# Two packed attentions and a gated convolution: transposes of batches 0 and 1 on TensorE, low words on VectorE, one more column for the 1e-9

## The chip, the cores and the metric

The kernel runs on one core of a Trainium2 chip. The metric is the device time of the program in microseconds, the median of the timed runs. Five engines work beside each other, each through its own queue in order: TensorE (PE in the profile, its weight loads PEld), VectorE (DVE), ScalarE (ACT), GpSimd (POOL) and SyncE (SP), which issues all transfers here. Work waits for other engines through semaphores.

## The reference

```python
def _attn_ref(q, k, v, p):
    scale = 1.0 / np.sqrt(q.shape[-1])
    def sm_attn(qq, kk, vv):
        s = scale * np.matmul(qq, kk.transpose(0, 1, 3, 2))
        s = s - np.max(s, axis=-1, keepdims=True)
        a = np.exp(s)
        a = a / (np.sum(a, axis=-1, keepdims=True) + 1e-09)
        return np.matmul(a, vv)
    p_packed = sm_attn(p, k, v)
    return sm_attn(q, p_packed, p_packed)

def _moe_ref(x, w_val, conv_w, w_out):       # x: (batch, seq, heads * head_dim)
    ...
    for k in range(K):                       # K = 5 taps, causal
        gate_pre += conv_w[k][None, None, :] * xp[:, k:k + S, :]
    gate = 1.0 / (1.0 + np.exp(-gate_pre))
    return (gate * (x @ w_val) @ w_out)
```

q, k, v are (8 batches, 8 heads, 576 rows, 64), p is (8, 8, 32, 64), all float32. In the first attention the 32 rows of p ask k and v; in the second the 576 rows of q ask the 32 packed rows. The result, 576 by 512 for each batch, goes through a convolution of 5 taps and a sigmoid as the gate, times the product with `w_val`, and then through `w_out`. The three weights come as float64.

## The kernel before

Each batch goes through the same stages, each written as a generator that issues a few instructions and yields: `k` (`keys`: p and k turned so that head_dim lies on partitions), `a` (`attn_pack`: scores `s`, maximum `nb`, exponentials `a`, their transposes `at`, the product `pv` with v, and the packed rows `ppd`), `q` (`queries`), `p` (`packed_turned`: `ppT`), `s` (`attn_out`: scores, turned on VectorE to `t`, maximum `mx` over 32 packed rows, subtracted on GpSimd, exponential on ScalarE), `t` (`weighted`: sums, reciprocals `rs`, scaling on GpSimd, turned back to `a` of the second attention, split into a high part `a2h` and a low part `a2l`), `w` (`packed_values`: packed rows times `w_val`, split into `wph` and `wpl`), `x` (`mixed`: for batches 0 to 2 the whole convolution on TensorE with the tap products `kx`, for the others the attention's output `xp`), `g` (`gate`: for batches 3 to 7 four taps on VectorE, then tanh on ScalarE, into `sig`), `v` (`value`: `val` on TensorE, times the gate on VectorE, split into `gvh` on ScalarE and `gvl` on GpSimd) and `o` (`project`: the output `o` of 128 rows in 12 matmuls, evicted to `osb` and stored).

Capital letters are loads (`K`, `Q`, `V`, `P`, and `L` for the weights) and the weights' preparation: `from_double` takes the words of a float64 apart on ScalarE, VectorE and GpSimd; `W` makes `wv`, `O` makes `woh` and `wol`, `C` the taps `cw` and their spread form `cwb`.

What is issued in which order is a table of tokens, `ORDER` (lines 48 to 71): `a2.2` takes two steps of batch 2's `attn_pack`. The class `InOrder` (lines 74 to 95) keeps each engine's instructions in that order. So an engine stands still when the first instruction of its queue waits, whatever is behind it. The `|` in the table marks where the buffers for the weights' words are given up and `gvh` and `gvl` take their place; 3 PSUM tiles (`big`) of two banks serve scores, transposes and values, and one bank each `mid` and `out`.

k and q are turned by VectorE in blocks of 32 by 32, two instructions of 1152 columns for each; so head_dim is split in two halves of 32, and a score is two matmuls of 32 rows that accumulate:

```python
                            of(rows, j, h),
                            xT[j // 2][rows, j % 2, :, h, :],
                            start=(h == 0),
                            stop=(h == 1),
```

The 1e-9 is added to each sum by VectorE (line 468), from a constant tile `eps`.

## Time and profile before

| | us |
|---|---|
| timed runs | 299.49, 299.0, 297.74; median 299.0 |
| the profiled execution | 301.0 |
| its span, first to last instruction | 299.2 |
| busy: PE, PEld, DVE, ACT, POOL | 259.6, 192.0, 245.2, 164.4, 124.6 |
| mean granted clock of TensorE | 0.945 |
| read from HBM, written | 33.57 MB, 9.44 MB |

In the rows of the profile, `L82` is the line of the helper that issues all instructions, so the tiles' names tell the groups apart. A row of a group has the engine, the operation, output<-inputs, the shapes, the count, the busy time with the mean of one in ns, and the engine's idle time before them with what ended it. A row in order of time has the start and the duration in us; `x12` is 12 instructions in one row. An instruction's duration can contain the time in which it was held up.

### The profile page before, as it was taken

What the parts mean: (1) busy time and instruction counts of PE and PEld (TensorE: products, weight loads), DVE (VectorE), ACT (ScalarE), POOL (GpSimd) and SP (SyncE); (2) the same over time, 40 slices, a digit from 0 to 9 for tenths busy, and PEclk for the clock granted to TensorE, in tenths of its full rate; (3) what the DMA queues carried; (4) which work ended last, traced back from release to release, by engine and by line L of the source; (5) the groups of instructions that cost most, each with busy time, mean ns of one, the idle gap of its engine ahead of it and who ended that gap; (6) DMA issues with size and microseconds to landing.
All of it is one profiled execution on the core that took longest, in us unless ns stands there. A gap on an engine that the chain in (4) does not pass through costs nothing.

```text
span 299.2 us, 8542 instructions
## 1 busy us (share of the span) xinstructions
PE 259.6 (87%) x3676; PEld 192.0 (64%) x3676; DVE 245.2 (82%) x349; ACT 164.4 (55%) x306; POOL 124.6 (42%) x107
## 2 busy tenths in 40 slices
PE   0465555989999998999999999999999979999984
PEld 0143343457677874768776768867876758778852
DVE  1499569799977898687999999999999989847841
ACT  4155345576753564477573766657764637546412
POOL 1334358659916474314424741541522803511230
PEclk9998555899999999999999999999999979999998
DMA  7999996534952498355467511565010101111004
GB/s 219 303 334 265 271 278 200 149 84 157 290 160 70 142 298 226 95 144 156 139 169 196 184 37 46 184 163 183 37 71 37 38 35 70 62 45 70 35 2 175
DMA packets 25839, 43.56 MB, mean 146 GB/s; under 512 B 5829, under 2 KB 11973, under 8 KB 25802
## 3 DMA queue, kind: packets, MB, share of 16 engines
q1 hardware_dynamic: 25802, 43.02, 48.6%
q8 instruction: 29, 0.48, 0.7%
q14 instruction: 8, 0.07, 0.1%
HBM read 33.57 MB, written 9.44 MB: 144 GB/s over the span
## 4 chain that ended last, share of the span: by engine, by line
PE 56%; DVE 23%; DMA 9%; ACT 5%; issue 3%; SPq 2%; POOL 1%; POOLq 1%; ACTq 0%; DVEq 0%
PE o L82 23%; DVE sig L82 13%; PE val L82 11%; PE x L82 8%; PE s L82 5%; DMA vm<-in_v_dram 3%; PE pv L82 3%; DMA wo_words<-in_moe_w_out_dram 3%; PE at L82 3%; DMA km<-in_k_dram 2%; DVE sm L82 2%; DVE kT L82 2%; SPq L82 2%; PE wp L82 1%; ACT sig L82 1%
## 5 line engine op out<-in xcount | busy, mean ns | idle before, releaser
L82 DVE SCALAR_TENSOR_TENSOR sig<-xp,cw,sig 128x576 f32<-128x576 f32 x80 | 76.5, 957 | 8.7 <-ACT sig L82 7.2
L82 POOL TENSOR_TENSOR gvl<-sig,gvh 128x576 fp32r<-128x576 f32 x32 | 48.4, 1514 | 79.7 <-ACT gvh L82 79.7
L82 PE MATMUL o<-woh,gvh 128*128 128x512 f32 x144 | 59.0, 410 | 2.8 <-ACT osb L82 2.7
L82 PE MATMUL o<-woh,gvl 128*128 128x512 f32 x144 | 57.3, 398 | 1.0 <-POOL gvl L82 1.0
L82 PE MATMUL o<-wol,gvh 128*128 128x512 f32 x144 | 56.9, 395 | 0.0
L82 PE MATMUL val<-a2h,wph 128*128 128x288 f32 x128 | 39.6, 310 | 0.0
L82 PE MATMUL val<-a2h,wpl 128*128 128x288 f32 x128 | 37.8, 295 | 0.0
L82 PE MATMUL val<-a2l,wph 128*128 128x288 f32 x128 | 37.7, 294 | 0.0
L82 ACT COPY osb<-o 128x512 f32<-128x512 f32 x34 | 19.9, 587 | 31.4 <-PE o L82 25.2
L82 PEld LDWEIGHTS o<-woh,gvh 128*128 128x128 f32 x144 | 27.4, 190 | 15.0 <-ACT osb L82 6.3
L82 PEld LDWEIGHTS o<-woh,gvl 128*128 128x128 f32 x144 | 27.3, 190 | 8.3 <-POOL gvl L82 2.1
L82 DVE SCALAR_TENSOR_TENSOR sig<-sig,val 128x576 f32<-128x576 f32 x32 | 23.7, 740 | 9.9 <-PE val L82 5.6
L82 PEld LDWEIGHTS o<-wol,gvh 128*128 128x128 f32 x144 | 27.5, 191 | 4.8
L82 POOL TENSOR_TENSOR t<-t,mx 128x576 f32<-128x576 f32 x16 | 20.8, 1299 | 19.5 <-DVE mx L82 19.4
L82 PE MATMUL pv<-vm,a1t 96*32 96x64 f32 x768 | 16.7, 239 | 13.9 <-ACT a1t L82 8.0
L82 POOL TENSOR_TENSOR t<-t,rs 128x576 f32<-128x576 f32 x16 | 20.6, 1288 | 17.7 <-DVE rs L82 15.0
L82 PEld LDWEIGHTS pv<-vm,a1t 96*32 96x32 f32 x768 | 13.4, 121 | 22.5 <-ACT a1t L82 14.4
L82 PE MATMUL s<-kT,pT 32*32 32x288 f32 x512 | 17.2, 479 | 12.1 <-DVE kT L82 11.7
L82 ACT CAST gvh<-sig 128x576 fp32r<-128x576 f32 x32 | 21.5, 673 | 10.5 <-DVE sig L82 9.4
L82 PEld LDWEIGHTS val<-a2h,wph 128*128 128x128 f32 x128 | 24.1, 188 | 5.0 <-DVE sig L82 1.4
L82 PEld LDWEIGHTS val<-a2h,wpl 128*128 128x128 f32 x128 | 24.1, 188 | 0.4
L82 PEld LDWEIGHTS val<-a2l,wph 128*128 128x128 f32 x128 | 24.1, 188 | 0.0
(81 smaller groups left out, 457.7 us busy)
## 6 DMA issues: line engine op xcount, KB each, us to landing
km<-in_k_dram SPq DMA_DIRECT2D x16, 576.0 KB, 6.1
vm<-in_v_dram SPq DMA_DIRECT2D x16, 576.0 KB, 7.1
qm<-in_q_dram SPq DMA_DIRECT2D x16, 576.0 KB, 5.3
out_dram<-osb SPq DMA_DIRECT2D x36, 256.0 KB, 2.1
wv_words<-in_moe_w_val_dram SPq DMA_DIRECT2D x4, 512.0 KB, 5.9
wo_words<-in_moe_w_out_dram SPq DMA_DIRECT2D x4, 512.0 KB, 10.2
p<-in_p_dram SPq DMA_DIRECT2D x16, 64.0 KB, 3.5
cw_words<-in_moe_conv_w_dram SPq DMA_DIRECT2D x1, 20.0 KB
```

What stands on the lines that cost most here:

```text
L82: made = getattr(self.engine, op)(*args, **kw)
```

## The change

It has six parts.

1. k, q and p of batches 0 and 1 (`BY_PE`) are loaded over all 128 partitions, 16 partitions for each head and one packet of 4608 B for each partition, and turned by TensorE: 3 groups of 12 transposes for each tensor into a `big` PSUM tile, each group copied to the two tiles `kT` or `qT` by two copies on ScalarE. p is loaded with each head's 64 columns twice and takes 2 transposes and one copy. VectorE's transposes of these tensors go away.
2. Since head_dim now lies whole on 64 partitions, the scores of batches 0 and 1 are one matmul of 64 rows each (`scores_by_64`), the first half of the heads before the second. Their `ppd` is written in one instruction instead of two, and `ppTt` has 2 transposes instead of 3.
3. The two sums of the first attention lie in one tile, so one add and one reciprocal serve both, after both exponentials.
4. `t` has a 33rd column, set to 1e-9 by GpSimd; the sum runs over 33 columns, and the add of `eps` goes away (all batches).
5. `gvl` of batches 3 to 7 is made by VectorE, not GpSimd. The factor 0.5 of `w_out` moves to the eviction of the output; in the weights' preparation the subtraction that gives `wo_top` moves from VectorE to GpSimd.
6. The table `ORDER` is another one throughout.

Diff, cut to its core (a line of "..." is left out):

```diff
+BY_PE = (0, 1)
+ON_POOL = {'al': (0, 1, 2), 'gvl': (0, 1, 2)}
 ORDER = """
-L0 W0 P0 L0 P0 W0.2 k0 K0 W0 k0 K0 W0 L0 W0 V0 K1 W0 k0 a0 W0.2 a0.4 W0 a0.3 W0.3 K1 k1 W0 a0 k1 a0 L0 Q0 W0 k1 L0
+L0 W0 K0 W0.3 P0.2 W0 K0 W0 L0 k0 W0 Q0 W0 k0.3 W0 k0.5 W0 k0 W0 k0 a0 W0 k1 W0 L0 W0 V0 W0 a0 q0 W0 a0 k1 a0.2 L0 K1
...
     def load(b, nm, src):
...
+            if b in BY_PE:
+                at = src[b].rearrange("h (i m) d -> (h i) m d", i=NP // 2)
+                m = m.rearrange("a j (m d) -> a (j m) d", d=D)
+                sp.dma_start(m, at[:, S // NP * n : S // NP * n + S // NP])
...
     def out_weights(b):
...
-            act.mul(hi, top, 0.5)
-            yield
-            dve.scalar_tensor_tensor(
-                top, top, 0.5, hi.bitcast(F32), op0=ALU.mult, op1=ALU.subtract
-            )
+            act.copy(hi, top)
+            yield
+            pool.tensor_tensor(top, top, hi.bitcast(F32), op=ALU.subtract)
...
+    def transposed_by_pe(b, nm):
+        parts = st[f"{nm}T", b] = []
+        for g in range(G):
+            parts.append(tile_of(f"{nm}T", [P, 4, HS], F32, f"{nm}T_{b}_{g}"))
+        for part in range(NPART):
+            pt = big(f"{nm}pt_{b}_{part}").rearrange("x u m -> x (u m)")
+            pt = pt.rearrange("x (h m) -> x h m", h=H)[:, :, : NP // 2 * NB6]
+            for n in range(NB6):
+                half, at = divmod(part * NB6 + n, S // NP // 2)
+                m = st[nm, b][half].rearrange("a j x -> a (j x)")
+                for u in range(2):
+                    rows = slice(64 * u, 64 * u + 64)
+                    pe.transpose(
+                        pt[:, 4 * u : 4 * u + 4, 16 * n : 16 * n + 16],
+                        m[rows, 2 * D * at : 2 * D * at + 2 * D],
+                        ident[rows, rows],
+                    )
+            yield
+            for g in range(G):
+                to = parts[g].rearrange("x j (i p n) -> x p j i n", p=NPART, i=NP // 2)[:, part]
+                ot = pt.rearrange("x (j g) m -> x g j m", g=G)[:, g]
+                act.copy(to, ot.rearrange("x j (n i) -> x j i n", i=NP // 2))
+                yield
...
+    def scores_by_64(name, of, xT):
+        two = [big(f"{name}_{e}")[:, :, :HS] for e in range(G)]
+        for e in range(G):
+            for j in range(4):
+                for c in range(2):
+                    rows = slice(D * c, D * c + D)
+                    pe.matmul(
+                        two[e][heads[j], c, :], of(rows, j, e), xT[e][rows, j, :], start=True, stop=True
+                    )
+        return two
...
     def attn_out(b):
-        t2 = st["t2", b] = tile_of("t2", [P, G, NBLK, NP], F32, f"t2_{b}")
+        t2 = st["t2", b] = tile_of("t2", [P, G, NBLK, NP + 1], F32, f"t2_{b}")
+        pool.memset(t2[:, :, :, NP:], 1e-9)
...
     def weighted(b):
...
-            dve.tensor_reduce(s3, t3, axis=AX.X, op=ALU.add)
-            dve.tensor_tensor(s3, s3, eps[:, : n * NBLK], op=ALU.add)
-            dve.reciprocal(r3, s3)
+            dve.tensor_reduce(r3, t3, axis=AX.X, op=ALU.add)
+            dve.reciprocal(r3, r3)
...
     def value(b):
...
-            pool.tensor_tensor(
+            (pool if b in ON_POOL["gvl"] else dve).tensor_tensor(
                 lo, gv, hi.bitcast(F32), op=ALU.subtract
...
     def project(b):
...
-                act.copy(osb, ops)
+                act.mul(osb, ops, 0.5)
```

Three places of the order, in the words of the two programs. The first is TensorE's queue at the start, from the transposes `at` of batch 0 to its query scores (`kpt` and `qpt` are the new transposes of k and q, `s` scores, `pv` the product with v, `ppTt` the turning of the packed rows; the first number behind a tile's name is the group, half or batch's part, the last its buffer). Before:

```order
L82 MATMUL at_0_165<-ident,a_0_0_152 96x64 x12
L82 MATMUL pv_0_187<-vm_0_106,a1t_0_164 32x64 x24
L82 MATMUL at_1_234<-ident,a_0_1_157 96x64 x12
L82 MATMUL s_1_0_256<-kT_0_212,pT_184 32x288 x2
...
L82 MATMUL pv_1_299<-vm_1_229,a1t_1_233 32x64 x24
L82 MATMUL ppTt_343<-ident,ppd_161 128x128 x3
L82 MATMUL at_0_353<-ident,a_1_0_296 96x64 x12
L82 MATMUL s_0_0_368<-qT_0_254,ppT_347 32x288 x2
```

and now:

```order
L85 MATMUL qpt_0_191<-ident,qm_0_100 128x4x16 x12
L85 MATMUL at_0_223<-ident,a_0_0_205 96x64 x12
L85 MATMUL kpt_0_244<-ident,km_0_215 128x4x16 x12
L85 MATMUL pv_0_261<-vm_0_183,a1t_0_222 32x64 x24
L85 MATMUL kpt_1_290<-ident,km_0_215 128x4x16 x6
L85 MATMUL kpt_1_290<-ident,km_1_237 128x4x16 x6
L85 MATMUL at_1_308<-ident,a_0_1_211 96x64 x12
L85 MATMUL kpt_2_323<-ident,km_1_237 128x4x16 x12
...
L85 MATMUL qpt_2_360<-ident,qm_1_239 128x4x16 x12
L85 MATMUL pv_1_408<-vm_1_353,a1t_1_307 32x64 x24
L85 MATMUL ppTt_436<-ident,ppd_221 128x128 x2
L85 MATMUL s_0_0_453<-qT_0_189,ppT_446 32x288 x8
```

Six groups of transposes (`qpt_0`, `kpt_0` to `kpt_2`, `qpt_1` and `qpt_2`; those of `qpt_1` and the first scores of batch 1 are in the part left out) now stand ahead of batch 0's second `pv`, where there were none; the three of `kpt` turn the keys of batch 1. On SyncE's queue, in the same stretch, the loads from the first half of batch 0's v (`vm_0`) to its second half (`vm_1`); before:

```order
L82 DMA vm_0_106<-in_v_dram 96x4x384
L82 DMA km_0_108<-in_k_dram 128x2x576
L82 DMA km_1_182<-in_k_dram 128x2x576
L82 DMA wv_words<-in_moe_w_val_dram 128x1024
L82 DMA qm_0_217<-in_q_dram 128x2x576
L82 DMA cw_words<-in_moe_conv_w_dram 5x1024
L82 DMA vm_1_229<-in_v_dram 96x4x384
```

and now:

```order
L85 DMA vm_0_183<-in_v_dram 96x4x384
L85 DMA wv_words<-in_moe_w_val_dram 128x1024
L85 DMA km_0_215<-in_k_dram 128x1152
L85 DMA cw_words<-in_moe_conv_w_dram 5x1024
L85 DMA km_1_237<-in_k_dram 128x1152
L85 DMA qm_1_239<-in_q_dram 128x1152
L85 DMA wo_words<-in_moe_w_out_dram 128x1024
L85 DMA vm_1_353<-in_v_dram 96x4x384
```

The second half of v now stands behind the second half of q and the first block of `wo_words` as well.

The second place is GpSimd's queue from batch 0's tap products `kx` to the second half of its `a2l`. Before:

```order
L82 TENSOR_TENSOR kx_551<-ppd_161,cwb 128x640
L82 TENSOR_TENSOR wv_words<-wv_words 128x512
L82 TENSOR_TENSOR wv<-wv_top,wv_words 128x512
L82 TENSOR_TENSOR wo_words<-wo_words 128x512
L82 TENSOR_TENSOR wol<-wo_top,wo_words 128x512
L82 TENSOR_TENSOR a2l_461<-a_0_459,a2h_460 128x576
```

and now:

```order
L85 TENSOR_TENSOR kx_640<-ppd_221,cwb 128x640
L85 TENSOR_TENSOR wv_words<-wv_words 128x512
L85 TENSOR_TENSOR wv<-wv_top,wv_words 128x512
L85 TENSOR_TENSOR wo_words<-wo_words 128x512
L85 TENSOR_TENSOR wo_top<-wo_top,woh 128x512
L85 TENSOR_TENSOR wol<-wo_top,wo_words 128x512
L85 TENSOR_TENSOR kx_718<-ppd_480,cwb 128x640
L85 TENSOR_TENSOR a2l_556<-a_0_554,a2h_555 128x576
```

The subtraction `wo_top<-wo_top,woh` is new here, and the tap products of batch 1 now stand ahead of `a2l`.

The third place is VectorE's queue in the last batch (`sig<-xp,cw,sig` is one tap, `sig<-sig,val` the product with the values). Before:

```order
L82 SCALAR_TENSOR_TENSOR sig_0_3605<-xp_0_3512,cw,sig_0_3605 128x576 x4
L82 SCALAR_TENSOR_TENSOR sig_0_3605<-sig_0_3605,val_0_3588 128x576
L82 SCALAR_TENSOR_TENSOR sig_1_3628<-xp_0_3512,cw,sig_1_3628 128x576 x4
L82 SCALAR_TENSOR_TENSOR sig_1_3628<-sig_1_3628,val_1_3634 128x576
L82 SCALAR_TENSOR_TENSOR sig_2_3668<-xp_1_3514,cw,sig_2_3668 128x576 x4
L82 SCALAR_TENSOR_TENSOR sig_2_3668<-sig_2_3668,val_2_3675 128x576
L82 SCALAR_TENSOR_TENSOR sig_3_3707<-xp_1_3514,cw,sig_3_3707 128x576 x4
L82 SCALAR_TENSOR_TENSOR sig_3_3707<-sig_3_3707,val_3_3741 128x576
```

and now:

```order
L85 SCALAR_TENSOR_TENSOR sig_0_3654<-xp_0_3574,cw,sig_0_3654 128x576 x4
L85 SCALAR_TENSOR_TENSOR sig_0_3654<-sig_0_3654,val_0_3660 128x576
L85 SCALAR_TENSOR_TENSOR sig_1_3692<-xp_0_3574,cw,sig_1_3692 128x576 x2
L85 TENSOR_TENSOR gvl<-sig_0_3654,gvh 128x576
L85 SCALAR_TENSOR_TENSOR sig_1_3692<-xp_0_3574,cw,sig_1_3692 128x576 x2
L85 SCALAR_TENSOR_TENSOR sig_1_3692<-sig_1_3692,val_1_3701 128x576
L85 SCALAR_TENSOR_TENSOR sig_2_3731<-xp_1_3576,cw,sig_2_3731 128x576
L85 TENSOR_TENSOR gvl<-sig_1_3692,gvh 128x576
L85 SCALAR_TENSOR_TENSOR sig_2_3731<-xp_1_3576,cw,sig_2_3731 128x576 x3
L85 SCALAR_TENSOR_TENSOR sig_2_3731<-sig_2_3731,val_2_3737 128x576
```

Each `gvl` of the last batch now stands between the next chunk's taps; the product with `val` still stands right behind its own taps.

More of the change, by code (lines that the diff above doesn't have):

```diff
@@ L71 @@
+v7.2 o7 v7 o7.15
 """
@@ L513, in mixed @@
             hc = slice(half * HS, half * HS + HS)
-            pp, a2 = st["ppd", b], st["a2", b]
+            pp, a2 = plain(b), st["a2", b]
             two = [big(f"x_{b}_{half}_{n}") for n in range(2)]
```

211 lines of the change are left out of this document (119 added, 92 removed).

## The prediction

> **What bounds the kernel now.** I read the windows by stage first, then the waits of TensorE, then the chain of waits, then the groups, and last the order of time at three places: the start, 240 us, and the tail.
>
> Busy time per stage (columns: engines with their instruction counts, granted clock, DMA share, GB/s):
>
> ```profile
> 0.00:61.50 61.50, 33.30 (x762) 19.97 (x762) 42.41 (x67) 29.44 (x58) 27.27 (x28) 0.78 0.91 251
> 61.50:79.20 17.70, 16.00 (x322) 11.70 (x316) 17.08 (x29) 11.78 (x23) 14.52 (x11) 1.00 0.52 152
> 79.20:140.00 60.80, 59.94 (x1162) 44.01 (x1163) 48.55 (x75) 35.50 (x76) 26.03 (x23) 1.00 0.57 165
> 140.00:240.00 100.00, 98.84 (x1167) 74.70 (x1165) 97.13 (x134) 61.41 (x109) 42.93 (x36) 1.00 0.38 117
> 240.00:266.00 26.00, 23.93 (x149) 19.23 (x142) 19.31 (x27) 14.91 (x24) 7.52 (x7) 0.93 0.16 61
> 266.00:299.20 33.20, 27.63 (x133) 22.37 (x131) 20.71 (x22) 11.38 (x18) 6.29 (x4) 0.97 0.17 64
> ```
>
> I cut at 61.5 us because the first matmul of `value` starts there. Before it TensorE works 33 of 61 us, at a low granted clock, and the DMA engines are 91% busy. From 79 to 240 us TensorE is 99% busy, and from 140 us VectorE is 97% busy beside it. In the last 33 us neither is. TensorE's waits from 61.5 us to the end (total, times, longest):
>
> ```profile
> PE o L82 <- ACT osb L82: 2.7, 2, 2.1
> PE pv L82 <- ACT a1t L82: 1.4, 2, 0.9
> PE o L82 <- POOL gvl L82: 1.0, 2, 0.8
> ```
>
> With the short ones these are some 7 us in 238. So after 61.5 us the kernel is bound by TensorE's work, which the change leaves as it is there (one batch's smaller score matmuls apart). Time can come from three places only: reaching the first `value` matmul sooner, the few stalls, and the tail.
>
> **Term 1, the start.** The rows of the start in order of time (start, duration, engine, operation; what the idle time before it waited for in brackets):
>
> ```profile
> 25.25 0.53 PE L82 MATMUL pv<-vm,a1t 96*32 96x64 f32 x21 [1.38 <-DMA vm<-in_v_dram]
> 29.42 0.90 PE L82 MATMUL at<-ident,a 64*96 64x64 f32 x12
> 30.24 2.59 PE L82 MATMUL s<-qT,ppT 32*32 32x288 f32 x64
> 43.42 0.77 DVE L82 STREAM_TRANSPOSE a<-t 128x576 f32<-128x576 f32 x1
> 48.43 1.54 POOL L82 TENSOR_TENSOR kx<-ppd,cwb 128x640 f32<-128x640 f32 x1
> 50.02 5.05 PE L82 MATMUL x<-a,kx 32*64 32x288 f32 x80 [0.62 <-POOL kx L82]
> 56.50 2.71 PE L82 MATMUL x<-a,kx 32*64 32x288 f32 x80
> 61.52 0.40 PE L82 MATMUL val<-a2h,wph 128*128 128x288 f32 x1
> ```
>
> Batch 0's chain runs: second half of v lands (25.25), its query scores (30.24), softmax and the turned-back `a` (43.42), the tap products (48.43), the convolution (50.02, at half clock: 5.05 us against 2.71 us for the same 80), the first `value` (61.52). Now the prices, from the groups:
>
> ```profile
> L82 DVE STREAM_TRANSPOSE qT<-qm 128x1152 f32<-128x1152 f32 x16 | 21.6, 1358 | 0.0
> L82 DVE STREAM_TRANSPOSE kT<-km 128x1152 f32<-128x1152 f32 x16 | 21.5, 1350 | 2.6 <-DMA km<-in_k_dram 2.5
> L82 ACT COPY ppT<-ppTt 128x384 f32<-128x384 f32 x8 | 3.8, 480 | 1.0 <-PE ppTt L82 1.0
> L82 DVE SCALAR_TENSOR_TENSOR wo_top<-wo_top,woh 128x512 f32<-128x512 f32 x4 | 3.7, 936 | 0.5 <-ACT woh L82 0.3
> L82 POOL TENSOR_TENSOR wol<-wo_top,wo_words 128x512 fp32r<-128x512 f32 x4 | 5.2, 1298 | 0.8 <-DVE wo_top L82 0.7
> ```
>
> - VectorE loses 8 transposes of k and q: 8 x 1.354 = 10.8 us, and 3.7 us of `wo_top`.
> - TensorE gains 12 groups of 12 transposes. The trace has none of this shape (64 rows by 128 columns); the nearest row is the 12 transposes of `at`, 0.90 us. So 12 x 0.90 = 10.8 us. From below, two thirds of it if half of each group overlaps better; from above 14.4 us, by 128 columns against 96. I take 10.8. Score matmuls over 64 rows are half as many: 16 row-and-column tiles become 8, and each takes one pass, not two. The work is equal if the array is full in both cases (2.59 us stays), half if the passes bind (1.3 us). I take 1.8 us, three times in the start: -2.4 us.
> - ScalarE gains 24 copies of 384 columns: 24 x 0.48 = 11.5 us, strided; the row of `ppT` is a plain one, so 11.5 is the lower end and 15 us an upper one.
> - GpSimd gains 4 subtractions of the `wo_top` shape, 4 x 1.30 = 5.2 us, and one short memset a batch.
>
> Each engine has room: 33 + 10.8 - 2.4, 29 + 11.5 and 27 + 4 us against 61. The cover for TensorE's transposes is its idle time before 50 us; if that is gone, each group costs its 0.9 us straight. The DMA order speaks against the change. The second half of batch 0's v is behind 1.1 MB more (the second q half and the first `wo` block): at 251 to 325 GB/s it lands 3.5 to 4.4 us later, about 29 us. The query scores then start near 32.5 instead of 30.24 us. But they come one half after the other, so VectorE can begin on the first half about 1 us after their start, 33.5 us against 32.84 before. Behind that, VectorE's queue no longer holds the k and q transposes. Before, `a` was ready only at 43.42, since VectorE stood behind other batches' work. Now I step through: first half subtracted, exponentiated, summed and scaled by 39.5 us (no add of 1e-9, no stop behind GpSimd); `a` behind the small `cw` copy, which waits for TensorE's `cwps`, at 40.7; then casts and tails on ScalarE and GpSimd (0.7 + 1.4), the second scaling and the tap product (1.2 + 1.54): the convolution starts at about 47.7 instead of 50.0. It lasts 5.05 us at half clock. Behind it GpSimd's queue decides: after the tap product it has two `wv` operations, one `wo` triple with the new subtraction, batch 1's tap product and `a2l`, some 9.4 us, so the low part of `a` is there at 57.1. The scores of batch 2 end at 58.5, and the first `value` is at 58.6 us: **-2.9**, and a half us more from the next stage, where GpSimd (14.5 of 17.7 us) has to finish two more triples before it may start on `gvl`. I take **-3.5 us**; bounds +6 (below) and -7.
>
> The clock: in this trace it was at half until the convolution had run for 5 us, though `s`, `pv` and transposes came before. [...]
>
> **Term 2, the middle.** The groups:
>
> ```profile
> L82 DVE SCALAR_TENSOR_TENSOR sig<-xp,cw,sig 128x576 f32<-128x576 f32 x80 | 76.5, 957 | 8.7 <-ACT sig L82 7.2
> L82 POOL TENSOR_TENSOR gvl<-sig,gvh 128x576 fp32r<-128x576 f32 x32 | 48.4, 1514 | 79.7 <-ACT gvh L82 79.7
> L82 DVE TENSOR_TENSOR a2l<-a,a2h 128x576 fp32r<-128x576 f32 x10 | 7.4, 745 | 0.8 <-ACT a2h L82 0.8
> L82 DVE TENSOR_TENSOR sm<-sm,eps 128x18 f32<-128x18 f32 x16 | 6.9, 434 | 0.6
> ```
>
> and the tail and 240 us in order of time:
>
> ```profile
> 235.50 5.41 DVE L82 SCALAR_TENSOR_TENSOR sig<-xp,cw,sig 128x576 f32<-128x576 f32 x4
> 240.95 0.68 ACT L82 ACTIVATE sig<-sig 128x576 f32<-128x576 f32 x1 [3.54 <-DVE sig L82]
> 242.16 0.50 PE L82 MATMUL o<-woh,gvh 128*128 128x512 f32 x1 [2.07 <-ACT osb L82]
> 265.93 3.38 DVE L82 SCALAR_TENSOR_TENSOR sig<-xp,cw,sig 128x576 f32<-128x576 f32 x4 [4.14 <-ACT sig L82]
> 270.10 0.75 DVE L82 SCALAR_TENSOR_TENSOR sig<-sig,val 128x576 f32<-128x576 f32 x1 [0.78 <-ACT sig L82]
> 270.77 4.63 DVE L82 SCALAR_TENSOR_TENSOR sig<-xp,cw,sig 128x576 f32<-128x576 f32 x4
> 271.64 1.43 POOL L82 TENSOR_TENSOR gvl<-sig,gvh 128x576 fp32r<-128x576 f32 x1 [8.55 <-ACT gvh L82]
> 285.87 0.50 PE L82 MATMUL o<-woh,gvl 128*128 128x512 f32 x1 [0.82 <-POOL gvl L82]
> 291.12 0.50 PE L82 MATMUL o<-woh,gvl 128*128 128x512 f32 x1 [0.18 <-POOL gvl L82]
> 292.30 0.50 PE L82 MATMUL o<-woh,gvh 128*128 128x512 f32 x1 [0.68 <-ACT osb L82]
> ```
>
> Four taps take 3.38 us when GpSimd is idle and 4.63 us when one `gvl` of 1.43 us runs beside them: GpSimd's operation holds the taps up for 1.25 us, nearly its own length. Over all 80 taps the excess is 80 x (0.957 - 0.845) = 9.0 us; about half belongs to `gvl`, half to GpSimd's softmax operations. So `gvl` of batches 3 to 7 on VectorE costs 20 x 0.745 = 14.9 us there, gives back some 4.5 us of held-up taps, and the adds of 1e-9 give back 10 x 0.434 = 4.3 us: **VectorE has about 6 us more** over batches 3 to 7, in a stage where it had 2.9 us of idle time in 100, then 6.7 in 26 and 12.5 in the last 33. That is the weak place of the change. Where the new order has `gvl` in the gap in which VectorE waited for ScalarE's tanh (0.78 us each time), it costs nothing; the order does so for most of them.
>
> At 240 us five things stand in a row: the taps are held up (5.41 instead of 3.38), tanh is late on ScalarE, the eviction of the output behind it is late, TensorE waits 2.07 us, and then its clock is down:
>
> ```profile
> 242.16 4.61 PE o L82 x12
> 248.35 2.76 PE o L82 x12
> ```
>
> Together 2.07 + 1.85 = 3.9 us on the path. The hold-up goes; but ScalarE's new queue again has a tanh ahead of an eviction there, so I count less than half: **-1.5 us**, bounds -4 and +4 (all of VectorE's 6 us but 2 on the path).
>
> **Term 3, the tail.** From the last pair of convolution sums, VectorE has four times 4 taps, a wait for tanh, the product with `val`; GpSimd the `gvl`. Without hold-up, four rounds lose 3 x 1.25 us and gain 3 x 0.67 us of `gvl`, and the last `gvl` is 0.7 us shorter: the tail of VectorE is 2.4 us shorter. TensorE is nearly dense beside it, and its waits there are 0.82, 0.18 and 0.68 us: the gain is bound by 1.7 us. I take **-1.2 us**, bounds 0 and -1.7. The factor 0.5, moved from the weights to the output's eviction, costs nothing: a scaled copy in place of a copy, on the same engine.
>
> **The sum.** -3.5 - 1.5 - 1.2 = -6.2 us. The profiled execution took 301.0 us with a span of 299.2 us; the median of the three timed runs is 299.0. I subtract from the median: 292.8, **293 us**.
>
> **The rivals.** (B) *The start gives nothing*: v's later landing and the transposes in TensorE's queue ahead of batch 0's chain eat what VectorE saves, the first `value` stays at 61.5. For it: the DMA share of 0.91; against: `a` at 43.42 was late through VectorE's queue. 299.0 - 1.5 - 1.2 = 296.3. [...] (D) *Slower: the start is bound by TensorE and ScalarE.* Six groups of transposes stand in TensorE's queue ahead of the second half of batch 0's `pv`: 6 x 0.9 on TensorE, and each pair of copies (0.96 us) must free a PSUM buffer before the next group. If these run behind v's landing rather than before it, 5.4 us come on top of v's 4, less the 3 us that VectorE's shorter queue gives back: +6, so 299.0 + 6 - 2.7 = 302.3 us. It decides from where batch 0's query scores start after 36 us. (E) *VectorE sets the pace from 140 us*: its 6 extra us cancel the start's gain: 299 - 1.2 + 1 = 298.8, no change.
>
> **Chances.** Forecast 0.42, B 0.20, C 0.15, D 0.13, E 0.10. The likeliest one's own range is 290 to 296. The range reaches to C's better end, 285.5, and to 300.5, which leaves D out. About 0.5% is what a measurement here can tell from no change, 297.5 to 300.5 us. Faster by more: forecast 0.41, C 0.15, B 0.15, E 0.01: 0.72. Same: B 0.05, E 0.08, and 0.01 of the forecast: 0.14. Slower: D and 0.01 of E: 0.14.
>
> **What would show it.** Right: the first `value` between 57 and 60 us; batch 0's query scores at 31 to 33.5 us; four taps of the tail in about 3.4 us; VectorE 2 to 6 us busier from 140 us on; no 2 us wait of TensorE near 240. [...] For D: those scores after 36 us, with TensorE waiting for ScalarE's copies. For E: TensorE waiting on VectorE for more than 5 us between 140 and 266. The forecast is wrong in its base if the first `value` comes at 61 us or later and the total still falls, or comes early and the total stays.

## The result, and the profile after

The changed kernel takes 295.88 us (median; 295.17 to 296.36) against 299.25 us of the kernel before beside it: a ratio of 0.9886, 95% interval 0.9846 to 0.9926. That is 3.4 us or 1.1% faster. The forecast was 293.0, range 285.5 to 300.5. So the sign and the range hold, and a little over half of the forecast gain came. What matters more is where it came from, and there the forecast was wrong in its largest term. Medians here are of all runs and ratios of the fast runs alone (those within 1.5% of a kernel's fastest), so a ratio need not be the quotient of two medians. The rows below come from single executions: that of the changed kernel took 295.72 us, that of the kernel before 301.0, which is 1.8 us above its median. So the rows part the two kernels by 5.3 us, and the medians by 3.4.

The windows of the changed kernel by stage, cut as those of before, at its own first `value` (61.2 us) and first `o` (78.5):

```profile
0.00:61.20 61.20, 36.38 (x813) 25.06 (x813) 34.12 (x50) 39.17 (x82) 34.03 (x33) 0.85 0.89 260
61.20:78.50 17.30, 16.45 (x300) 12.63 (x296) 16.79 (x25) 11.17 (x22) 13.18 (x13) 0.95 0.66 191
...
140.00:240.00 100.00, 99.60 (x1209) 74.97 (x1208) 97.25 (x137) 63.49 (x113) 25.27 (x26) 1.00 0.34 103
240.00:266.00 26.00, 25.98 (x163) 21.27 (x162) 20.68 (x29) 14.13 (x24) 1.31 (x3) 1.00 0.16 60
266.00:293.90 27.90, 23.38 (x110) 18.82 (x109) 16.47 (x22) 10.17 (x16) 0.00 (x0) 1.00 0.20 76
```

The first stage is as long as before, 61.2 against 61.5 us, though VectorE works 34 us in it in place of 42. From 140 us on TensorE is busy nearly all the time (it was 98.84 of 100 and 23.93 of 26), at the full clock, and GpSimd has little left to do. The first and last start of an `o` matmul say it in two numbers, first before, then after:

```profile
L82 PE MATMUL o<-woh,gvh x144: 389/393/628, 79.1 to 294.5; 128*128 128x512 f32 x144
```

```profile
L85 PE MATMUL o<-woh,gvh x144: 391/398/505, 78.5 to 289.2; 128*128 128x512 f32 x144
```

Between these two executions the change gains 0.6 us up to the first `o`; from there to the last one it gains 215.4 - 210.7 = 4.7 us. Where the 1.8 us lie by which the execution of the kernel before was above its median, the rows do not show, so both gains may be smaller in the median. Another execution with the start of the kernel before (the run with `gvl` on VectorE in the old order, below) has its first `o` at 78.6 us, as late as the changed kernel's 78.5.

The start of the changed kernel in order of time, TensorE's rows from 31 us (start, duration, engine, operation; idle time before it and what ended it in brackets):

```profile
31.63 0.31 PE L85 MATMUL pv<-vm,a1t 96*32 96x64 f32 x4 [0.94 <-ACT a1t L85]
32.90 0.86 PE L85 MATMUL pv<-vm,a1t 96*32 96x64 f32 x44 [0.96 <-issue]
33.70 0.82 PE L85 MATMUL at<-ident,a 64*96 64x64 f32 x12
34.45 0.41 PE L85 MATMUL cwps<-ident,cw_top 5*128 5x5 f32 x4
34.78 1.31 PE L85 MATMUL spread<-cw_top,ident 5*32 5x64 f32 x67
40.69 0.64 PE L85 MATMUL spread<-cw_top,ident 5*32 5x64 f32 x13 [4.59 <-issue]
...
47.36 5.17 PE L85 MATMUL x<-a,kx 32*64 32x288 f32 x80 [2.48 <-POOL kx L85]
...
59.02 2.24 PE L85 MATMUL s<-kT,pT 32*32 32x288 f32 x64 [2.37 <-DVE wpl L85]
```

Two things hold it up. In the middle of `spread`, the 40 matmuls that lay out the taps (80 records in the profile, which shows each of them as two; a transpose is one record), TensorE stands still for 4.59 us, and the profile names nothing that it waits for ("issue"). The copy of `spread` to `cwb`, the tap product `kx` and the convolution stand behind that. Later it waits 2.37 us for `wpl`, behind work on VectorE that runs beside a GpSimd that is busy without a gap (5.92 of the 6 us from 51.5). VectorE's rows in order of time:

```profile
51.69 1.47 DVE L85 TENSOR_SCALAR wo_words<-wo_words 128x512 uint32<-128x512 uint32 x1
53.27 1.59 DVE L85 SCALAR_TENSOR_TENSOR wo_top<-wo_top,wo_words 128x512 uint32<-128x512 uint32 x1
54.90 1.68 DVE L85 TENSOR_SCALAR wo_words<-wo_top 128x512 uint32<-128x512 uint32 x1
...
57.78 1.19 DVE L85 TENSOR_TENSOR wpl<-wp,wph 128x1024 fp32r<-128x1024 f32 x1
```

In the kernel before, VectorE's rows of the same three operations in order of time, at 58.56 to 60.24 us, while GpSimd stood idle (from 58.08 to 60.38):

```profile
58.56 0.42 DVE L82 TENSOR_SCALAR wo_words<-wo_words 128x512 uint32<-128x512 uint32 x1
59.09 0.69 DVE L82 SCALAR_TENSOR_TENSOR wo_top<-wo_top,wo_words 128x512 uint32<-128x512 uint32 x1
59.81 0.43 DVE L82 TENSOR_SCALAR wo_words<-wo_top 128x512 uint32<-128x512 uint32 x1
```

In the middle and the tail, the groups on VectorE (count | busy us, mean ns of one | idle time before) and four taps and a `gvl` of the tail:

```profile
L85 DVE SCALAR_TENSOR_TENSOR sig<-xp,cw,sig 128x576 f32<-128x576 f32 x80 | 65.6, 821 | 5.6 <-ACT sig L85 4.7
...
L85 DVE TENSOR_TENSOR gvl<-sig,gvh 128x576 fp32r<-128x576 f32 x20 | 15.8, 788 | 1.5 <-ACT gvh L85 1.5
```

```profile
266.58 1.67 DVE L85 SCALAR_TENSOR_TENSOR sig<-xp,cw,sig 128x576 f32<-128x576 f32 x2
268.17 0.75 DVE L85 TENSOR_TENSOR gvl<-sig,gvh 128x576 fp32r<-128x576 f32 x1
268.84 1.67 DVE L85 SCALAR_TENSOR_TENSOR sig<-xp,cw,sig 128x576 f32<-128x576 f32 x2
```

A tap takes 821 ns in place of 957, 10.9 us less over 80. `gvl` stands between taps and waits 1.5 us in all. VectorE's busy time from 62 us to the end did not grow by 6 us, as the forecast had it for batches 3 to 7; it fell from 202.28 to 199.83 us (the third busy time in the rows of that window, before first):

```profile
62.00:310.00 248.00, 225.84 (x2913) 171.52 (x2911) 202.28 (x282) 134.49 (x248) 97.30 (x79) 0.99 0.37 113
```

```profile
62.00:310.00 248.00, 224.78 (x2881) 170.94 (x2879) 199.83 (x274) 134.69 (x246) 66.60 (x65) 1.00 0.36 110
```

### The profile page after: what moved, and what is told of

It is laid out like the page before. It is cut to its first block, busy times and chain, and to the rows that moved or that the text cites. A ratio compares the mean times of both kernels' runs of the same rounds, so it can differ in the third digit from the quotient of the medians.

```text
span 293.9 us, 8560 instructions
## 1 busy us (share of the span) xinstructions
PE 262.0 (89%) x3694; PEld 196.8 (67%) x3694; DVE 234.8 (80%) x323; ACT 173.9 (59%) x328; POOL 100.9 (34%) x98
## 4 chain that ended last, share of the span: by engine, by line
PE 74%; DVE 9%; DMA 5%; issue 4%; ACT 3%; POOL 3%; SPq 0%; DVEq 0%; POOLq 0%; ACTq 0%
PE o L85 36%; PE val L85 17%; PE s L85 6%; PE x L85 6%; DMA km<-in_k_dram 3%; PE pv L85 3%; PE at L85 3%; PE wp L85 2%; DVE wo_words L85 2%; DVE kT L85 2%; DMA p<-in_p_dram 2%; DVE wo_top L85 2%; POOL t L85 1%; PE ppTt L85 1%; ACT a L85 1%
## 5 line engine op out<-in xcount | busy, mean ns | idle before, releaser
L85 DVE SCALAR_TENSOR_TENSOR sig<-xp,cw,sig 128x576 f32<-128x576 f32 x80 | 65.6, 821 | 5.6 <-ACT sig L85 4.7
L85 ACT ACTIVATE osb<-o 128x512 f32<-128x512 f32 x34 | 20.3, 596 | 30.5 <-PE o L85 26.9
L85 POOL TENSOR_TENSOR t<-t,mx 128x576 f32<-128x576 f32 x16 | 21.5, 1344 | 27.1 <-DVE mx L85 26.5
L85 POOL TENSOR_TENSOR gvl<-sig,gvh 128x576 fp32r<-128x576 f32 x12 | 17.7, 1477 | 24.7 <-ACT gvh L85 24.5
L85 ACT ACTIVATE sig<-sig 128x576 f32<-128x576 f32 x20 | 13.7, 685 | 13.3 <-DVE sig L85 13.1
L85 PE MATMUL x<-a,kx 32*64 32x288 f32 (+4 forms) x480 | 19.1, 451 | 2.5 <-POOL kx L85 2.5
L85 PE MATMUL s<-kT,pT 32*32 32x288 f32 (+1 forms) x448 | 14.7, 454 | 6.2 <-ACT kT L85 2.9
```

The lines of the kernel that those rows point to most:

```text
L85: made = getattr(self.engine, op)(*args, **kw)
```

## The experiments

The questions: which part of the change makes the gain behind the first `o`, and why the start gave next to nothing. Ratios are against the kernel before, run beside them on the same chip.

| kernel | median us | before beside it | ratio (95%) |
|---|---|---|---|
| changed kernel | 295.88 | 299.25 | 0.9886 (0.9846 to 0.9926) |
| changed kernel, once more | 295.86 | 299.18 | 0.9824 (0.9766 to 0.9882) |
| gvl all on GpSimd | 298.26 | 299.18 | 0.9944 (0.9904 to 0.9984) |
| wo_top on VectorE | 296.49 | 299.18 | 0.9924 (0.9891 to 0.9956) |
| spread by 20 matmuls | 291.03 | 299.18 | 0.9736 (0.9701 to 0.9771) |
| without the TensorE part | 293.93 | 299.50 | 0.9809 (0.9779 to 0.9840) |
| same, spread by 20 | 293.74 | 298.84 | 0.9809 (0.9770 to 0.9847) |
| spread by 20, adds of 1e-9 back | 293.40 | 298.84 | 0.9808 (0.9767 to 0.9849) |
| spread by 20, wpl earlier | 291.03 | 299.50 | 0.9721 (0.9683 to 0.9759) |
| 40 transposes more at the start | 294.02 | 298.84 | 0.9795 (0.9744 to 0.9846) |
| before, gvl of b > 2 on VectorE | 305.39 | 299.50 | 1.0205 (1.0170 to 1.0239) |
| same, with the 33rd column | 303.78 | 299.10 | 1.0147 (1.0098 to 1.0195) |
| before, spread by 20 | 297.09 | 299.50 | 0.9923 (0.9893 to 0.9953) |

### The changed kernel once more

> The changed kernel once more, as the yardstick for the runs beside it. Both theories: 295.9 us, give or take 0.5; the stall of TensorE inside the matmuls of spread (4.59 us before) is again there, between 3 and 6 us, after 67 of the 80; first value matmul near 61 us.

295.86 us, as expected; but its single executions spread from 291.5 to 298.1 us, and its second ratio lies just outside the first one's interval (the two intervals overlap). The first `value` came at 63.0 us in the profiled execution, not near 61. The stall stands at the same record, at another length, as TensorE's rows in order of time show:

```profile
42.23 0.64 PE L85 MATMUL spread<-cw_top,ident 5*32 5x64 f32 x13 [3.48 <-issue]
```

I read nothing out of differences of under 1.5 us between kernels that have this stall.

### gvl of all batches on GpSimd

```diff
-ON_POOL = {'al': (0, 1, 2), 'gvl': (0, 1, 2)}
+ON_POOL = {'al': (0, 1, 2), 'gvl': range(8)}
```

> The changed kernel with gvl of all batches on GpSimd, in the same order. Theory G (the gain behind the first value, 4.6 us of TensorE's end, comes from gvl leaving GpSimd): the 80 taps take 0.93 to 0.97 us each again instead of 0.82, four taps of the tail that run beside a gvl take about 4.6 us instead of 3.4, a wait of TensorE of 1.5 us or more comes back, and the time is 298.5 to 301 us, about that of the kernel before. Rival R (the gain comes from the other order and from the adds of 1e-9 that are gone): taps slower, but hidden, the time stays within 0.7 of 295.9 us.

298.26 us, 2.4 us more than the changed kernel by the medians: theory G in its mechanism, just below the size it gave (298.5 to 301). The interval of its ratio lies above that of the changed kernel beside it, but overlaps that of the changed kernel's first measurement. The taps are slow again, by the groups:

```profile
L85 DVE SCALAR_TENSOR_TENSOR sig<-xp,cw,sig 128x576 f32<-128x576 f32 x80 | 78.2, 977 | 6.3 <-ACT sig L85 5.2
```

and the matmuls of `o`, with the first and the last start:

```profile
L85 PE MATMUL o<-woh,gvh x144: 391/397/505, 76.6 to 289.8; 128*128 128x512 f32 x144
```

From the first to the last `o` it takes 213.2 us against 210.7. The wait of 1.5 us that the theory expected did not come; the longest wait for another engine in that stretch is 0.7 us.

This execution showed something else. TensorE's program is the same as the changed kernel's up to the convolution, and in its rows in order of time no stall without a name stands here:

```profile
36.88 2.36 PE L85 MATMUL spread<-cw_top,ident 5*32 5x64 f32 x80
...
45.48 4.03 PE L85 MATMUL x<-a,kx 32*64 32x288 f32 x80 [2.69 <-POOL kx L85]
...
58.94 0.61 PE L85 MATMUL val<-a2h,wph 128*128 128x288 f32 x1
```

So the stall is no fixed cost of the program, and without it the first `value` comes at 58.94 us.

### wo_top back on VectorE

```diff
-            pool.tensor_tensor(top, top, hi.bitcast(F32), op=ALU.subtract)
+            dve.tensor_tensor(top, top, hi.bitcast(F32), op=ALU.subtract)
```

> The changed kernel with the subtraction of wo_top on VectorE again (4 operations of about 0.7 to 0.9 us there, 1.26 us each off GpSimd). Theory H (GpSimd's additional operations hold VectorE up between 47 and 62 us): VectorE's uint32 operations there take 1.0 to 1.3 us instead of 1.4 to 1.7, wpl of batch 0 starts 1 to 2.5 us before 57.8, the first value is at 59 to 60.3 us, and the time is 294 to 295.3 us. Rival S (VectorE has about as much to do either way): the hold-up gets less, but the added 4 x 0.7 us cancel it; first value between 60.5 and 62, time 295.3 to 297 us.

296.49 us: rival S, by the total. The hold-up does get less, `wo_top<-wo_top,wo_words` takes 1046 ns in place of 1302 in the mean, but the four operations of 672 ns are back in the queue ahead of `wpl`, and TensorE waits longer for it, 4.55 us. The groups:

```profile
L85 DVE SCALAR_TENSOR_TENSOR wo_top<-wo_top,wo_words 128x512 uint32<-128x512 uint32 x4 | 4.2, 1046 | 0.8 <-DVE wo_words L85 0.5
...
L85 DVE TENSOR_TENSOR wo_top<-wo_top,woh 128x512 f32<-128x512 f32 x4 | 2.7, 672 | 0.1
```

The first `value` comes at 64.4 us in this execution, later than either side had it; at 298.35 us it is one of the longest of this kernel, and it has the stall in `spread` as well (4.38 us). The move of this subtraction to GpSimd costs VectorE about what it saves, and the time does not tell the two apart.

### spread by 20 matmuls

```diff
-        spread = big("spread")[:, :, : NT * D]
-        for g in range(G):
-            for kk in range(NT):
-                for j in range(4):
-                    pe.matmul(
-                        spread[heads[j], g, kk * D : kk * D + D],
+        spread = big("spread").rearrange("a g x -> a (g x)")
+        for kk in range(NT):
+            for j in range(4):
+                pe.matmul(
+                    spread[heads[j], kk * G * D : kk * G * D + G * D],
...
-                        taps[:, (2 * j + g) * D : (2 * j + g) * D + D],
+                    taps[:, 2 * j * D : 2 * j * D + G * D],
...
-        act.copy(cwb.rearrange("a g k d -> a g (k d)"), spread)
+        spread = spread[:, : NT * G * D].rearrange("a (k g d) -> a g k d", k=NT, g=G)
+        act.copy(cwb, spread)
```

> The changed kernel with spread made by 20 matmuls of 128 columns in place of 40 of 64 (40 matmul records in place of 80, the same values). Theory I (TensorE's instructions arrive in blocks, about 127 matmul records apart, and the wait for a block is long while the loads fill the DMA engines): the stall keeps its place in the count of records, so it lands behind spread, about 27 records into the 36 transposes of batch 1's queries; the copy cwb ends by 39 us instead of 42.1, the first tap product (kx) starts at 41.5 to 43.5 instead of 45.8, the convolution at 43.5 to 45.5 instead of 47.4; first value 58 to 60 us, time 293 to 295 us. Rival J (the stall belongs to spread itself or to a moment in time): it stays inside spread or at its end, convolution at 47 or later, time 295.5 to 296.4. Rival K (the count is right, but GpSimd's and VectorE's queues decide behind it): convolution by 45.5, first value still past 60.3, time 295.2 to 296.2.

TensorE's rows in order of time:

```profile
36.33 2.36 PE L85 MATMUL spread<-cw_top,ident 5*32 5x128 f32 x40
38.62 1.75 PE L85 MATMUL qpt<-ident,qm 64*128 64x64 f32 x27
41.94 0.70 PE L85 MATMUL qpt<-ident,qm 64*128 64x64 f32 x9 [1.57 <-issue]
...
44.77 5.17 PE L85 MATMUL x<-a,kx 32*64 32x288 f32 x80 [0.69 <-POOL kx L85]
...
58.57 0.61 PE L85 MATMUL val<-a2h,wph 128*128 128x288 f32 x1
```

Theory I, to the very record: the stall moved to 27 records into the 36 transposes, 44 + 12 + 4 + 40 + 27 = 127 records behind the one in `pv`, as it had been 44 + 12 + 4 + 67 = 127 behind it. `spread` itself is no shorter: 40 records of 128 columns take the 2.36 us that 80 records of 64 took in the kernel above. What changes is that `cwb` no longer stands behind the stall: the convolution starts at 44.8 us, the first `value` at 58.6. The time, 291.03 us, is below the expected 293 to 295: no kernel of the study is faster, and it is 2.6% below the kernel before.

The start is only part of that. In this execution the first `o` comes at 75.9 us, 2.6 us before the changed kernel's, and from there to the last one it takes 208.7 us in place of 210.7. The changed kernel has one more stall without a name in that stretch, of 1.33 us near 124 us, which this execution has not. The execution is the slowest of its kernel's six all the same, 293.06 us: its last eviction ends at 286.1 us and the span at 291.3, so 5.2 us behind it, against 3.2 us in the changed kernel.

### Without the TensorE part, and the same with the smaller spread

`BY_PE` is empty; VectorE turns k, q and p of batches 0 and 1 in blocks of 32 x 32 at about the places that the new order gives the turning.

```diff
-BY_PE = (0, 1)
+BY_PE = ()
...
+            if b < 2:
+                yield
+                yield
```

> The changed kernel without its TensorE part: k, q and p of batches 0 and 1 are transposed by VectorE in 32 x 32 blocks again, with loads, 32-row scores and copies as before, each at about the place that the new order gives it. Theory L (the turning by TensorE is worth something in the start): VectorE has 8 transposes of about 1.35 us more before 50 us, the convolution starts at 48 us or later, the first value at 62 or later, TensorE's granted clock stays at half until the convolution, the time is 297 to 299.5 us. Rival M (it is worth nothing there, since the loads and the stall of TensorE set that time): convolution at 46 to 48, first value at 60 to 61.8, time 294.8 to 296.6 us.

293.93 us: lower than theory L and than rival M. As built, the TensorE part costs about 2 us by the medians (295.9 to 293.9), though the changed kernel's second ratio, 0.9824, is not told apart from the 0.9809 here. VectorE has its 8 transposes again, and the convolution starts at 46.5 us all the same, 3.5 us earlier than in the kernel before: the other parts of the change do that, the new order among them. The first `value` is at 61.00 us, as in the changed kernel, and the only stall without a name that TensorE's waits list in this execution is one of 1.14 us (rows in order of time).

```profile
42.62 1.49 PE L85 MATMUL pv<-vm,a1t 96*32 96x64 f32 x44 [1.14 <-issue]
46.50 5.08 PE L85 MATMUL x<-a,kx 32*64 32x288 f32 x80 [2.38 <-POOL kx L85]
```

So most of the 2 us is not in the start: the first `o` comes 0.6 us earlier than in the changed kernel (77.9 us), and from there to the last one it takes 208.7 us, without the stall near 124 us.

Is turning by TensorE worth nothing, or is its worth eaten by the stall? The smaller `spread` without the TensorE part tells:

> The changed kernel without its TensorE part (k, q, p of batches 0 and 1 by VectorE) and with spread by 20 matmuls. Counted in matmul records, the block boundary at 475 stays in the pv behind spread (44 records in, after 4 before). Theory T (turning by TensorE is worth 2 to 3 us, and the stall in spread had eaten it): this kernel stays near the one without the TensorE part, 293 to 294.6 us, so 2 to 3.5 us behind the 291.0 of the changed kernel with the smaller spread. Rival U (the smaller spread gives about 2.5 to 5 us in any of these kernels, and turning by TensorE gives nothing): 290 to 291.6 us.

293.74 us, no change from 293.93: theory T. Beside 291.03 of the changed kernel with the smaller `spread`, the TensorE part is worth 2.7 us where the stall stands off the path (the two intervals just touch), with the first `value` at 58.57 against 60.90 us and the last `o` at 284.6 against 286.5. Where the stall stands in `spread`, that worth is lost, and by the medians more.

### Forty transposes more at the start

```diff
             pt = one(f"pTt_{b}")
+            for n in range(40 if b == 0 else 0):
+                pe.transpose(pt[:64, :64], ident[:64, :64], ident[:64, :64])
```

> The changed kernel with 40 additional transposes of the identity on TensorE at its very start, where it waits 7.6 us for p; their output is overwritten. Theory I (blocks of 127 to 128 matmul records): each stall stands 40 records earlier in the program: the one in spread after 27 of its 80 records in place of 67, the one before it 8 records into batch 0's query scores in place of 4 records into pv, none at 10 of 12 in the transposes near 124 us. Time 295 to 298 us. Rival J (the stalls belong to these operations, or to a moment in time): they stay at 67 of 80 and 4 of 48, 295.5 to 296.5 us.

294.02 us, below the 295 to 298 of theory I, and the stalls are in part as it has them. No stall stands at 67 of 80, and none at 27 of 80 either; the first one that shows is in `pv`, by TensorE's rows in order of time:

```profile
37.22 2.35 PE L85 MATMUL spread<-cw_top,ident 5*32 5x64 f32 x80
39.51 2.19 PE L85 MATMUL qpt<-ident,qm 64*128 64x64 f32 x36
42.31 1.29 PE L85 MATMUL pv<-vm,a1t 96*32 96x64 f32 x39 [0.62 <-DMA vm<-in_v_dram]
44.22 0.48 PE L85 MATMUL pv<-vm,a1t 96*32 96x64 f32 x9 [0.62 <-issue]
```

Counted from the start, that is 601 records in: 446 up to `cwps` with the 40 new ones, then 80 + 36 + 39. In the changed kernel the stalls stand at 346 and 473. 601 is 128 behind 473: the stalls stand on one grid of 127 to 128 records, but not at each of its points. The expectation was wrong in taking each point for a stall.

Later in the program it was right. The changed kernel's stall near 124 us stands 2 records into 12 transposes; here one stands 27 records into the 64 of `s` right ahead of these transposes, so 39 records earlier, about the number that was added (the changed kernel first):

```profile
124.04 0.72 PE L85 MATMUL at<-ident,a 64*96 64x64 f32 x10 [1.33 <-issue]
```

```profile
121.56 1.37 PE L85 MATMUL s<-kT,pT 32*32 32x288 f32 x37 [1.49 <-issue]
```

### gvl on VectorE in the old order, alone and with the 33rd column

```diff
-            pool.tensor_tensor(
+            (pool if b < 3 else dve).tensor_tensor(
                 lo, gv, hi.bitcast(F32), op=ALU.subtract
```

> The kernel before with one part of the change alone: gvl of batches 3 to 7 on VectorE, in the old order. Theory G: the 80 taps take 0.82 to 0.85 us each instead of 0.957, four taps of the tail 3.4 us, TensorE's wait of 2.07 us near 242 us gets shorter than 1 us, the time falls by 1.5 to 3.5 us, to 295.7 to 297.7. Rival E (VectorE's additional 15 us set the pace from 140 us on): VectorE busy for over 98 of 100 us there, waits of TensorE for sig or gvl of 3 us or more together, time 298.5 to 301 us.

305.39 us: slower by 5.9 us, more than rival E's 298.5 to 301. Taps are faster, 874 ns, but not as fast as 821; `gvl` waits 4.6 us for its `gvh`; VectorE has 210.22 us of work from 62 us on in place of 202.28, and TensorE, with 94.26 us of work in the 100 us from 140, falls behind. VectorE is busy 96.50 us of these 100, not over 98 as rival E had it: the order makes it wait. The window:

```profile
140.00:240.00 100.00, 94.26 (x1118) 69.54 (x1117) 96.50 (x136) 59.04 (x104) 22.88 (x22) 1.00 0.37 113
```

and the groups:

```profile
L82 DVE SCALAR_TENSOR_TENSOR sig<-xp,cw,sig 128x576 f32<-128x576 f32 x80 | 69.9, 874 | 6.7 <-ACT sig L82 5.6
...
L82 DVE TENSOR_TENSOR gvl<-sig,gvh 128x576 fp32r<-128x576 f32 x20 | 15.9, 795 | 4.7 <-ACT gvh L82 4.6
```

Then the adds of 1e-9 were taken away too, in the old order:

```diff
-        t2 = st["t2", b] = tile_of("t2", [P, G, NBLK, NP], F32, f"t2_{b}")
+        t2 = st["t2", b] = tile_of("t2", [P, G, NBLK, NP + 1], F32, f"t2_{b}")
+        pool.memset(t2[:, :, :, NP:], 1e-9)
...
-            dve.tensor_tensor(s3, s3, eps[:, : n * NBLK], op=ALU.add)
```

> The kernel before, in its old order, with two parts of the change: gvl of batches 3 to 7 on VectorE, and 1e-9 as a 33rd column in place of the 16 adds. With gvl alone it took 305.4 us, against 299.5 before. Theory X (VectorE's load sets the pace in the old order, so that each microsecond taken off it counts): the 16 adds of 0.43 us less give back 3 to 5 us, 300.5 to 302.5 us, and the new order is worth the 6 to 8 us that are left to the 293.9 of the changed kernel without its TensorE part. Rival Y (it is where the old order puts gvl, behind its gvh of the same tile, that costs): the adds give 1 us or less, 304.2 to 305.5 us, and the new order is worth 10 to 11.5.

303.78 us: 1.6 us less, between the two expectations, and the intervals of the two kernels overlap. So moving 20 operations to VectorE in the old order loses, and taking 16 small ones off does not mend it. What lies between this kernel and the 293.93 of the changed one without its TensorE part, 9.9 us, is the new order, with the joint sums of the first attention (part 3) and the moves of `wo_top` and of the factor 0.5, of which the move of `wo_top` showed no gain above. These were not parted further, so how much is the order's own is not shown. What its trace shows is the 821 against 867 to 874 ns of a tap, and 1.5 against 4.6 to 5.0 us of waits for `gvh`.

### The adds of 1e-9 put back

```diff
-        pool.memset(t2[:, :, :, NP:], 1e-9)
+        pool.memset(t2[:, :, :, NP:], 0.0)
...
+            dve.tensor_tensor(r3, r3, eps, op=ALU.add)
```

> The changed kernel with spread by 20 matmuls, and the adds of 1e-9 on VectorE again (16 small operations of 0.43 us in the kernel before; the 33rd column holds 0 and is still summed). Theory V (VectorE's time counts nearly in full in batches 3 to 7, as the forecast's 4.3 us had it): 292.5 to 295 us. Rival W (in the new order VectorE's work is hidden behind TensorE, which is 99% busy): 290.7 to 292 us.

293.40 us, 2.4 us above the same kernel without them by the medians (the two intervals just touch): theory V. The first `o` is at the same time (76.0 against 75.9 us), and from there to the last one it takes 210.5 us in place of 208.7: 1.8 us of it show there. VectorE's work in the new order still sets part of the pace, though TensorE is 99% busy beside it from 140 to 240 us.

### wpl earlier

```diff
-w0 O0 V2.2 x0 O0.2 k2 O0.2 K3 p1 O0 w0.2 O0 x0
+w0 O0 V2.2 x0 w0.2 k2 O0.2 O0.2 K3 p1 O0 O0 x0
```

> The changed kernel with the 20 matmuls of spread, and three steps moved in its order: wph and wpl of batch 0, and the second transpose of batch 2's keys, ahead of the last step of the third output weight block on VectorE. Theory P (the 2.4 us that TensorE waits for wpl are the place of that step behind held-up work): wpl starts 2 to 3 us earlier, the wait falls below 1.3 us, first value at 56.8 to 57.7 us, time 289.3 to 290.3. Rival Q (the weight blocks behind it then come late): the wait falls, but o of batch 0 waits for wol, time 290.7 to 292.

291.03 us, the same as without the three moved steps and so in rival Q's range. The wait for `wpl` is down to 0.19 us, as theory P had it, and the first `value` is at 56.10 us in place of 58.57: from the start of the convolution (44.65) it now takes 11.5 us. But behind it, and not at rival Q's `wol`, TensorE waits 2.07 us for the exponentials of batch 2, and the first `o` is only 0.9 us earlier. TensorE's rows in order of time:

```profile
53.34 0.68 PE L85 MATMUL s<-kT,pT 32*32 32x288 f32 x4 [0.19 <-DVE wpl L85]
...
60.03 0.82 PE L85 MATMUL at<-ident,a 64*96 64x64 f32 x12 [2.07 <-ACT a L85]
```

### The smaller spread in the kernel before

> The kernel before with spread made by 20 matmuls of 128 columns. Theory I (what the smaller spread gave in the changed kernel was the place of the stall): in the kernel before the stall of 3.1 us stands ahead of spread, in pv, and TensorE waits 5.8 us for a1t behind it, so 40 records fewer change nothing on the path: 299.2 us, give or take 1. Rival N (the smaller spread is itself faster, whatever stands where): 295 to 298 us.

The edit is that of the smaller `spread` above. 297.09 us, 2.4 us less than before: rival N by the number, and the expectation was wrong. By the trace `spread` is no shorter, 2.36 us again, and TensorE waits 5.78 us for `a1t` behind it as before. The stalls without a name stand elsewhere or are shorter (0.83 us in `pv` in place of 3.09, and three of 0.70 to 1.60 us between 62 and 90 us), and the profiled execution is the slowest of this kernel, 300.0 us. The rows do not account for the 2.4 us; this stays open. Without the TensorE part the same edit changed nothing (293.74 against 293.93), so a smaller `spread` is not faster as such; but how much of the 4.9 us in the changed kernel comes from other causes than the place of the stalls is not shown.

## Why the prediction was right or wrong

**Term 1, the start (forecast -3.5; measured -0.3 at the first `value`, -0.6 at the first `o`): wrong.** The forecast's own test says so: it called itself wrong in its base if the first `value` came at 61 us or later and the total still fell, and it came at 61.2. Rival B's outcome is the one that came, in the start and in the total (296.3 against 295.9), but not for rival B's reasons: v came earlier, and what the start lost it lost to a stall and to VectorE's queue.

- *v's second half at about 29 us, the query scores near 32.5:* wrong. The scores started at 28.73 us. The DMA engines moved 312 GB/s in the first 26 us in place of 288, and the 48 matmuls of `pv` ran from 26.28 us with no wait.
- *The prices:* 12 transposes at 0.90 us were too dear: 36 took 2.18 us at 8.15 us, and 2.19 at 41.26, where the granted clock was 0.50, so 0.73 us for each twelve. The 64-row scores at 1.8 us stand between the 2.18 at 13.2 us and the 1.20 at 28.7. 24 copies at 0.48 us: right (483 and 489 ns). TensorE's rows of the changed kernel:

```profile
8.15 2.18 PE L85 MATMUL kpt<-ident,km 64*128 64x64 f32 x36
13.23 2.18 PE L85 MATMUL s<-kT,pT 64*32 64x288 f32 x32 [2.89 <-ACT kT L85]
...
22.19 0.54 PE L85 MATMUL kpt<-ident,km 64*128 64x64 f32 x12
...
28.73 1.20 PE L85 MATMUL s<-qT,ppT 64*32 64x288 f32 x32 [0.46 <-ACT ppT L85]
```

- *The convolution at about 47.7 us, at half clock for 5.05 us:* 47.36 and 5.17, right by luck, since errors cancel: v was earlier, and the stall of 4.59 us, which the sum did not have at all, put it back. The sum does not close either: its terms from `a` at 40.7 us (0.7 + 1.4, 1.2 + 1.54) end at 45.5, and 2.2 us of the 47.7 stand in no term. The rows of before had shown such stalls, 1.42 and 3.09 us "issue" in `pv`. I read past them as a fixed part of the start; they are not. In the old order they stood off the path: with 0.69 us of stall there in place of 4.5, another execution of the same start had its first `value` at 61.0 us. A change that adds or takes records ahead of them in TensorE's program puts them at other operations: 40 fewer moved one from `spread` into the transposes of q, and 40 more moved one from `at` near 124 us into the `s` ahead of it.
- *GpSimd's queue decides behind the convolution, first `value` 10.9 us after its start:* it took 13.8. The step that failed is that only GpSimd's queue was followed. VectorE's operations beside it took 1.5 to 1.7 us in place of 0.4 to 0.7, and `wpl` in that queue was the last to come. With `wpl` earlier in that queue the stretch took 11.5 us, so it was this queue that decided. That a busy GpSimd makes VectorE's operations long is read from the rows side by side; no run took GpSimd's work away there altogether. Giving GpSimd the four subtractions was counted as GpSimd's price alone; with them back on VectorE the time is the same.

Where the stall stands off the path (58.57 us) or does not come (58.94), the first `value` is where the forecast had it, 58.6, but again by luck: the convolution starts at 44.8 us, earlier than the 47.7 of the forecast, and takes 13.8 us to the first `value` in place of 10.9. The total with the stall off the path is 291.0, 4.9 us below the changed kernel, of which the rows show 2.6 us in the start.

**Term 2, the middle (forecast -1.5), and term 3, the tail (-1.2): the sign right, the size too small in the rows** (4.7 us against 2.7; by the medians, which differ by only 3.4 in all, it may have been about right). The price that was mis-sized is that of the held-up taps: -4.5 us in the sum, 10.9 measured, of which 6.6 come with `gvl` alone in the old order (957 to 874 ns) and the rest with the new one. With the adds of 1e-9 that makes VectorE 2.4 us less busy in place of 6 more, and the 2 us wait near 240 us is gone (25.98 us of work in 26). The adds were sized at 4.3 us of VectorE's time; putting them back costs 2.4 us of the total by the medians and 1.8 between the first and the last `o`. Putting `gvl` back costs 2.5 there. Together that is 4.3 us, close to the 4.7. The tail's four taps take 3.34 us, as forecast (3.4). The factor 0.5 costs next to nothing, as forecast: an eviction takes 596 ns in place of 587 on ScalarE and 692 as before on VectorE.

The weak place that the forecast named was the right one. That VectorE would pay for `gvl` depends on where the order puts it: in the old order the move costs 5.9 us, more than rival E gave it; in the new one, with the other parts of the change, taking it back costs 2.4 by the medians. So the forecast's sentence "the order does so for most of them" carried far more of the result than the price of the operations, and no row of the trace stood behind it.

**The other rivals.** C has the clock up before the convolution and a total of 285.5 us at best: half of it came. The prices did fall early: twelve transposes took 0.54 us at 22.2 us in place of 0.90 at 18.6, and 32 records of 64-row scores 1.20 us at 28.7 in place of 2.18 at 13.2. But behind the stall of 4.59 us the granted clock was 0.50, and the convolution took 5.17 us, so C's gain did not come. A high granted clock ahead of the convolution (0.85 in the first stage, 0.78 before) is a weak sign of C: in the kernel before the column reads 1.00 from 12 to 16 us, where 48 records of `s` take 2.46 us, while at 60 us 60 of them take 1.57. D: the query scores were earlier, not later: not D. E did not come true in the new order.

**Transposes and the clock.** The forecast had the convolution at half clock, 5.05 us. So it was in the changed kernel, 5.17 us with a granted clock of 0.52 from 47 to 53 us, but after lower prices had come among the transposes and gone with the stall: the column reads 1.00 up to 34 us and 0.50 from 36 to 47. The lower prices began in a stretch that has 48 records of `pv` among the transposes; in the run with `wpl` earlier they began ahead of that `pv`, with twelve transposes in 0.59 us at 17.86 us after 0.91 for twelve at 15.86. The 40 transposes alone, 4.47 us without a gap, were followed by two transposes of p in 0.69 us, against 0.44 for two of the same shape at 51.0 us; but 1.83 us of idle time lie between them, and in the kernel before, too, 80 records of the convolution took 5.05 us before the next 80 took 2.71. So what brings the clock up is not shown.

## What to carry to other kernels

Do not take idle time that ends with "issue" for a fixed part of an operation. In this kernel it sat at a count of TensorE's records, 127 to 128 apart: where a change adds or removes instructions ahead of the critical path, count where those stalls land, and give that path fewer instructions if they land in it. When work moves to an engine that is nearly full, its own price can say little; what decided here was the order around it, and the same move gained in one order and lost in another. And when two engines hold each other up, sum the holding up over all that runs beside the moved operation, on both sides of the move.
